# A windowed attention with a gated convolution layer behind it: the whole hand-laid order of its engines replaced

## The chip, the core and the metric

One core of a Trainium2 chip runs the kernel. The metric is the device time of one execution in microseconds, as the median of several. The core's engines run side by side, each through its own row of instructions in order: TensorE (PE) multiplies matrices, VectorE (DVE), ScalarE (ACT) and GpSimd (POOL) do the elementwise work, and SyncE (SP) issues the transfers between the memory and the chip. An instruction waits until what it reads has been written and what it overwrites has been read; everything behind it on its engine waits with it.

## The reference

```python
B, H, S, D = 8, 8, 576, 64
window = 64
scores = 1 / sqrt(D) * (q @ k.transpose)
scores = where((0 <= i - j) & (i - j < window), scores, -1e9)
scores = scores - max(scores)
attn = exp(scores); attn = attn / (sum(attn) + 1e-9)
x = (attn @ v).transpose(0, 2, 1, 3).reshape(B, S, H * D)       # 8 x 576 x 512

xp = pad(x, 4 rows of zeros in front)
gate_pre = sum(conv_w[k] * xp[:, k:k + S] for k in range(5))    # each of 512 channels by itself
gate = sigmoid(gate_pre)
y = (gate * (x @ w_val)) @ w_out                                # 8 x 576 x 512, float32
```

## The kernel before

**Tiles.** Heads go in groups of four (two pairs of heads), so that 16 groups w = 0 to 15 make the eight batches, two to a batch. A query block has 32 rows and sees 96 keys; a group is done in two pieces, g = 0 with five blocks and g = 1 with four, each piece in two halves hh. The 128 partitions hold four pieces of 32 queries.

**Operations and their names.** Every operation has a name, and the prediction uses these. `S(w,g)` are the scores of a piece on PE (line 521, 80 or 64 matmuls into PSUM tiles `s`). `M((w,g),hh)` adds the mask and takes the maximum on DVE (line 542, one instruction for each block). `X` is the exponential with the sum on ACT (line 552, one for each block). `R(w,g)` adds the sums up and takes the reciprocal on DVE (lines 560 and 561). `N` multiplies by it (line 573 on POOL or DVE, line 571 on ACT). `T` transposes on DVE into `pts` (line 579). `AVw_0` to `AVw_10` are the products with v on PE (line 610, into `av`), `EXi` copies a pair of heads from `av` to `x` (line 241 on ACT, line 244 on DVE; pairs 2w and 2w+1 belong to group w), `XHi` rounds it to the multiplier's format and `XLi` (POOL, line 760) keeps the rest. The convolution of pair i is `Ci_4` on ACT (line 811) and then `Ci_3` to `Ci_0` on DVE (line 808), which add the other taps into `gp`. For the pairs 0 and 1 it is done on PE instead: `Ki_0` and `Ki_1` (line 777, with diagonal matrices `DG0`, `DG1`, line 975, that POOL makes), copied out by `CC`. `SIGb` is the sigmoid of a batch on ACT (line 995). `Vb_h_jb` are the products with `w_val` on PE (line 852; each as three products of a high and a low part), `HF` (line 863, DVE) multiplies by the gate, `HH` and `HL` split the result, `O` are the products with `w_out` on PE (line 918), `EO` copies the result out and `DO` stores it.

**Weights.** The weights come as raw 64-bit words and are turned into float32 parts on the chip: for each of eight words `w0` to `w7`, and for the convolution's `cw`, a chain of operations `h k b c H p l r s` (lines 413 to 469; `b` is line 424, `r` 451, `s` 454). The prediction calls these the number operations. They fall in the first 70 us, and they stand between the attention's operations on the same engines.

**The order.** Nothing is scheduled at run time. A table `ORDER` lists all operations as words, and the function `placed` takes them in that sequence, with the engine behind a slash where an operation may run on more than one: each engine's row is the table's words for that engine. A word `*a+b` puts a + b matmuls that compute nothing (the spares, lines 1032 and 1034) ahead of the next operation:

```python
for word in ORDER:
    if word[0] == "*":
        spares = tuple(int(x) for x in word[1:].split("+"))
        continue
    name, _, e = word.partition("/")
```

Two PSUM tiles `s` hold the two halves of one piece of scores, so that the next `S` has to wait for both `M` of the one before. Two tiles `av` hold one group's products, and two tiles are shared by `K`, `V` and `O`. Loads stand in SP's row: `LQ` for q and k of a pair, `LV` for v of a group (eight transfers), `LW` for weight words (0.5 MB for `w_val`'s halves, 1 MB for `LW2` and `LW3` of `w_out`).

Of the kernel before, what the change touches and what calls it, by code (L numbers as in the profile page):

```python
# [45 lines left out]
    low='NNNNNAAAA',  # L46
)
# [7 lines left out]
X((1,0),1) w4u w3l/V R(0,1) w4k/V *1+0 S(1,1) N((0,1),1)/G T((0,0),1) M((1,1),1) N((0,1),0)/G T((0,1),1) w4b
M((1,1),0) T((0,1),0) *0+1 AV0_0 AV0_1 AV0_2 w3r/G w4c w3s/V w4p LQ4_0 LW3 LQ5_0 LV1 LW0_1 LQ6_0 LQ7_0 AV0_3
AV0_4 AV0_5 AV0_6 AV0_7 AV0_8 AV0_9 AV0_10 *0+3 S(2,0) X((1,1),0) w4l/V X((1,1),1) R(1,0) R(1,1) EX0/V DG1/G
w5h/A w4H N((1,1),0)/A EX1/A XH0/A w5u XH1/A N((1,0),1)/V w4r/V N((1,0),0)/V w4s/V M((2,0),0) T((1,0),1)
T((1,0),0) M((2,0),1) N((1,1),1)/G XL1 DG0/G XL0 FR0 FR1 K1_0 AV1_0 S(2,1) T((1,1),1) T((1,1),0) M((2,1),0)
M((2,1),1) K1_1 AV1_1 AV1_2 AV1_3 AV1_4 X((2,0),0) X((2,0),1) w1h/A X((2,1),0) CC1_0 X((2,1),1) AV1_5 AV1_6  # L60
AV1_7 AV1_8 AV1_9 AV1_10 w1k/V R(2,0) w5k/V w1b w5b w1c N((2,0),0)/V w5c w1p w5p T((2,0),0) R(2,1) K0_1 S(3,0)
w1H CC1_1 EX2/A EX3/A C2_4 XH2/G C3_4 CC0_1 XH3/A N((2,0),1)/A w1l/V C2_3 M((3,0),0) C3_3 M((3,0),1) K0_0
T((2,0),1) C3_2 S(3,1) M((3,1),0) M((3,1),1) LV2 LQ8_0 LQ9_0 LV3 S(4,0) X((3,0),0) w5H w5l/G w1r/G XL3
N((2,1),1)/G XL2 w1s/G w5r/G w5s/G N((2,1),0)/G LQ10_0 LQ11_0 V0_1_1_0 X((3,0),1) X((3,1),0) CC0_0 X((3,1),1)
w6h/A w7h/A C2_2 C3_1 C2_1 R(3,0) C2_0 T((2,1),1) C3_0 N((3,0),1)/G N((3,0),0)/G M((4,0),0) T((2,1),0) R(3,1)
M((4,0),1) w6k/V w7k/V w6b w7b SIG0_0 w6c w7c HF0_1_1 w6p w7p FX1 FX0 AV2_0 AV2_1 AV2_2 AV2_3 AV2_4 AV2_5 AV2_6
AV2_7 AV2_8 AV2_9 AV2_10 V0_0_2_0 S(4,1) V0_0_3_0 T((3,0),1) HF0_0_2 M((4,1),1) HF0_0_3 T((3,0),0) EX4/A w6u
EX5/A C5_4 w7u C4_4 LV4 LQ12_0 LQ13_0 N((3,1),0)/G HH0_1_1_0/G HL0_1_1_0 w6l/G HH0_0_2_0/A HH0_0_3_0/A HL0_0_3_0
HL0_0_2_0 w7l/G V0_0_0_0 C4_3 M((4,1),0) HF0_0_0 C5_3 C4_2 X((4,0),0) w6H w7H V0_1_0_0 V0_0_1_0 S(5,0) HF0_1_0
# [1014 lines left out]
```

## Time and profile before

| | |
|---|---|
| median of 3 runs | 329.29 us (329.21 to 330.62) |
| the profiled execution's own time | 331.42 us |
| its span from first to last instruction | 329.6 us |
| PE busy | 313.0 us, 95% |
| DVE busy | 260.3 us, 79% |
| ACT busy | 246.0 us, 75% |
| POOL busy | 174.0 us, 53% |
| mean granted clock of TensorE | 0.979 |

The profiled execution is 2.1 us longer than the median, and 1.8 us of its own time lie outside its span. The views are read in this order: the slices of the span, to see where PE is full and where it is not; PE's waits in the full part; the chain of work that ended last; then, in the part where PE is not full, the timelines of DVE, ACT and POOL, where each row is an instruction or a merged run of them, with the idle time ahead of it and what ended that in square brackets.

### The profile page before, as it was taken

The page shows a single profiled execution, that of the slowest core. Times are in us where ns is not written, and L with a number is a line of the kernel's source. Part 1 is how long each engine was busy: PE and PEld are TensorE (multiplying, and loading weights), DVE is VectorE, ACT ScalarE, POOL GpSimd, SP SyncE. Part 2 cuts the span into 40 slices and gives each one's busy share as a digit, 9 for nine tenths or more (in the row PEclk, how much of TensorE's full clock was granted, in tenths as well). Part 3 has the DMA queues.
Part 4 walks back from the last instruction along what each step waited for, and adds up shares of the span by engine and source line. Part 5 has one row for each costly group of instructions (what it writes and reads, how often), then busy time and mean ns, then how long its engine had stood idle before and what let it go on. Part 6 is the DMA issues. An engine that isn't in the chain of part 4 may idle for free.

```text
span 329.6 us, 14996 instructions
## 1 busy us (share of the span) xinstructions
PE 313.0 (95%) x6142; PEld 264.2 (80%) x6142; DVE 260.3 (79%) x992; ACT 246.0 (75%) x844; POOL 174.0 (53%) x227
## 2 busy tenths in 40 slices
PE   8966978899999999999999999999999999999996
PEld 3435766799788988798889988798889888989985
DVE  5799977999989999999989897799886948572301
ACT  3688969999999799999987677949797467552110
POOL 3436428579849860279504895148147721671710
PEclk9976879999999999999999999999999999999999
DMA  7969884260156654664536335550433111010022
GB/s 229 384 131 291 254 234 136 96 196 33 37 177 196 193 169 122 184 183 152 148 126 191 110 105 189 183 157 2 140 114 116 30 69 64 34 66 32 2 96 95
DMA packets 28228, 45.03 MB, mean 137 GB/s; under 512 B 3968, under 2 KB 15488, under 8 KB 28160
## 3 DMA queue, kind: packets, MB, share of 16 engines
q1 hardware_dynamic: 28160, 44.08, 43.3%
q8 instruction: 48, 0.79, 1.0%
q14 instruction: 20, 0.16, 0.2%
HBM read 34.62 MB, written 9.44 MB: 134 GB/s over the span
## 4 chain that ended last, share of the span: by engine, by line
PE 80%; DVE 13%; ACT 5%; issue 2%; POOL 0%; ACTq 0%; POOLq 0%
PE o L918 29%; PE v L852 27%; PE av L610 10%; PE s L521 8%; DVE p L542 4%; DVE gp L808 3%; PE g L777 3%; PE spare L1032 2%; ACT p L552 2%; DVE pts L579 2%; ACT p L571 1%; ACT h_hi L241 1%; PE spare L1034 0%; DVE w4a L424 0%; ACT L552 0%
## 5 line engine op out<-in xcount | busy, mean ns | idle before, releaser
L552 ACT ACTIVATE p<-p,nm 128x96 f32<-128x96 f32 x288 | 103.9, 363 | 7.7 <-DVE nm L542 7.5
L808 DVE SCALAR_TENSOR_TENSOR gp<-av,cw,gp 128x575 f32<-128x575 f32 (+3 forms) x120 | 93.4, 802 | 7.5 <-ACT gp L811 6.7
L852 PE MATMUL v<-xl,wv_hi 128*128 128x288 f32 x256 | 77.6, 303 | 0.7 <-ACT ot L241 0.7
L852 PE MATMUL v<-xh,wv_lo 128*128 128x288 f32 x256 | 75.4, 294 | 0.0
L852 PE MATMUL v<-xh,wv_hi 128*128 128x288 f32 x256 | 75.0, 293 | 0.0
L881 POOL TENSOR_TENSOR h_lo<-hf,h_hi 128x288 fp32r<-128x288 f32 (+2 forms) x80 | 53.9, 690 | 23.5 <-ACT h_hi L241 22.0
L542 DVE CUSTOM_DVE_ANT_0 p<-s,mask 128x96 f32<-128x96 f32 x288 | 54.8, 250 | 7.3 <-PE s L521 7.1
L918 PE MATMUL o<-wo_hi,h_lo 128*128 128x512 f32 (+1 forms) x148 | 59.6, 403 | 0.2 <-DVE hf L863 0.2
L918 PE MATMUL o<-wo_lo,h_hi 128*128 128x512 f32 (+1 forms) x148 | 57.7, 390 | 0.0
L918 PE MATMUL o<-wo_hi,h_hi 128*128 128x512 f32 (+1 forms) x148 | 57.6, 389 | 0.0
L552 ACT ACTIVATION_READ_ACCUMULATOR p<-p,nm 128x1 f32 x288 | 54.2, 188 | 0.0
L852 PEld LDWEIGHTS v<-xl,wv_hi 128*128 128x128 f32 x256 | 48.1, 188 | 4.0 <-ACT ot L241 1.1
L760 POOL TENSOR_TENSOR xl<-x,xh 128x576 fp32r<-128x576 f32 x32 | 46.0, 1445 | 9.9 <-ACT xh L241 9.6
L246 POOL CAST h_hi<-hf 128x288 fp32r<-128x288 f32 (+2 forms) x37 | 14.2, 392 | 66.1 <-DVE hf L863 57.6
L852 PEld LDWEIGHTS v<-xh,wv_hi 128*128 128x128 f32 x256 | 48.2, 188 | 0.6
L852 PEld LDWEIGHTS v<-xh,wv_lo 128*128 128x128 f32 x256 | 48.1, 188 | 0.0
L610 PEld LDWEIGHTS av<-pts,v 32*64 32x64 f32 x2560 | 36.5, 135 | 11.3 <-issue 5.3
L610 PE MATMUL av<-pts,v 32*64 32x96 f32 (+2 forms) x2560 | 39.6, 251 | 6.1 <-DVE pts L579 2.7
L521 PEld LDWEIGHTS s<-ktb,qtb 64*32 64x32 f32 x2304 | 30.7, 108 | 17.4 <-issue 14.5
L521 PE MATMUL s<-ktb,qtb 64*32 64x96 f32 x2304 | 38.9, 255 | 5.2 <-issue 2.7
L863 DVE TENSOR_TENSOR hf<-v,gp 128x288 f32<-128x288 f32 x64 | 28.2, 447 | 18.0 <-PE v L852 13.9
L573 POOL TENSOR_TENSOR p<-p,rc 128x384 f32<-128x384 f32 (+1 forms) x30 | 28.5, 955 | 20.9 <-DVE rc L561 17.6
(129 smaller groups left out, 443.6 us busy)
## 6 DMA issues: line engine op xcount, KB each, us to landing
out_dram<-ot SPq DMA_DIRECT2D x35, 256.0 KB, 2.5
qtb<-in_qT_dram SPq DMA_DIRECT2D x30, 288.0 KB, 4.2
ktb<-in_kT_dram SPq DMA_DIRECT2D x30, 288.0 KB, 4.5
v<-in_vw_dram SPq DMA_DIRECT2D x64, 96.0 KB, 3.3
v<-in_vw_dram SPq DMA_DIRECT2D x64, 80.0 KB, 3.3
st<-in_w_val_dram SPq DMA_DIRECT2D x4, 512.0 KB, 4.1
st<-in_w_out_dram SPq DMA_DIRECT2D x2, 1024.0 KB, 10.2
qtb<-in_qT_dram SPq DMA_DIRECT2D x2, 224.0 KB
```

Source lines behind the costliest of these rows:

```text
L246: COPY = {"A": scopy, "V": vcopy, "G": lambda out, in_: nc.gpsimd.tensor_copy(out=out, in_=in_)}
L521: nc.tensor.matmul(sp_t[m, hh][z * Q:z * Q + Q, t, :], lhsT=held("qt", i)[r, c:c + Q], rhs=held("kt", i)[r, c:c + KW], start=True, stop=True)
L542: nc.vector.tensor_tensor_reduce(out=pe[:, t, :], in0=sp_t[u][:, t, :], in1=mask_of(w, n0 + t), scale=-SCALE, scalar=3.0e38, op0=ALU.add, ...
L552: nc.scalar.activation(out=pe[:, t, :], in_=pe[:, t, :], func=AF.Exp, scale=-1.0, bias=nm[:, t:t + 1], accum_out=su[:, t:t + 1])
L573: MUL[e](out=pe, in0=pe, in1=rc.unsqueeze(2).broadcast_to([P, ng, KW]))
L610: nc.tensor.matmul(av_t[w, z // 2][hh * D:(hh + 1) * D, c + lo * Q:c + hi * Q], lhsT=v_t[w][z * Q:z * Q + Q, hh, m % 2, m // 2 - KEYS[th][ ...
L760: SUB[e](out=batch_tile(xl_t, "xl", b, F32R)[:, hp, :], in0=x_t[i // 2][:, i % 2, :], in1=xh_t[b][:, hp, :].bitcast(F32))
L808: nc.vector.scalar_tensor_tensor(out=acc, in0=av(i, 0, S - back), scalar=col, in1=acc, op0=ALU.mult, op1=ALU.add)
L852: nc.tensor.matmul(vp_t[u][:, 0:NH], lhsT=w[:, c, js], rhs=x[:, c, hs], start=(a + z == 0), stop=(a + z == NM - 1))
L863: nc.vector.tensor_mul(out=hf, in0=vp_t.pop(u)[:, 0:NH], in1=gp_t[b][:, jb, hs])
L881: SUB[e](out=h_lo[:, jb, dst:dst + hi - lo], in0=hf_t[u][:, lo:hi], in1=h_hi[:, jb, dst:dst + hi - lo].bitcast(F32))
L918: nc.tensor.matmul(op_t[key][:, 0:cs.stop - cs.start], lhsT=h[:, jb, col:col + P], rhs=w[:, jb, cs], start=(a + z == 0), stop=(a + z == NM ...
```

## The change

`CFG` gets a line `lane=(2200.0, 900.0, 700, 3350, 1.15)`, which nothing in the code reads. The table `ORDER` is replaced as a whole: the same operations, in another sequence, some on other engines. All line numbers behind `CFG` are higher by one. Of the table's first lines:

```diff
+    lane=(2200.0, 900.0, 700, 3350, 1.15),
 ...
-LW1_0 LC LQ0_0 LQ1_0 *5+0 S(0,0) w2h/A w2k/V cwh/A cwk/V w2b cwb w2c cwc w2p cwp w2l/V cwl/V M((0,0),0)
+LW1_0 LC LQ0_0 LQ1_0 LW0_0 LW1_1 w2h/V LQ0_1 LQ1_1 w2k/V cwh/A cwk/V w2b cwb w2c cwc cwH w2H w2p cwp w2l/V LQ2_0
+*4+0 S(0,0) cwl/G M((0,0),0) X((0,0),0) w2r/G LQ3_0 M((0,0),1) w0h/V w0k/V w2s/V w0b X((0,0),1) *2+0 S(0,1) w0c
```

The spares ahead of the first scores become four instead of five, those ahead of `S(1,0)` one instead of four. Up to the product `HF0_1_1` (the first with the gate of batch 0), DVE loses `cwl`, `cws`, `w4l`, `EX0` and three `N` of five blocks, and gets `w2h`, `w2s`, `w3r`, `w6p`, `DG0` and `EX1`. Over the whole run `N` stands on ACT 20 times (19 before), on POOL 36 times (30) and on DVE 8 times (15). On SP the 1 MB load `LW3` moves from between `LQ4` and `LQ5` to behind `LV1`, so that `LQ5` comes earlier.

On DVE, ahead of the first mask operation of piece (1,0) (`p_1_0`, line 542, line 543 after), stood before:

```order
L433 TENSOR_SCALAR w0m<-w0a 128x512
L439 SCALAR_TENSOR_TENSOR w0l<-st_225,w0m 128x512
L420 TENSOR_SCALAR w3m<-w3m 128x512
L560 TENSOR_REDUCE rc_0_263<-sums_64 128x10
L561 RECIPROCAL rc_0_263<-rc_0_263 128x10
L424 TENSOR_SCALAR w3a<-w3m 128x512
L454 TENSOR_TENSOR cl<-cwm,cwl 128x20
L429 SCALAR_TENSOR_TENSOR w3a<-st_139,w3a 128x512
L542 ISA p_1_0_323,nm_1_0_322<-s_1_0_286,mask_91 128x96
```

In this row, `p_1_0_323` belongs to the second piece, and `w0`, `w3` and `cl` are number operations. After:

```order
L425 TENSOR_SCALAR w0a<-w0m 128x512
L430 SCALAR_TENSOR_TENSOR w0a<-st_146,w0a 128x512
L561 TENSOR_REDUCE rc_0_298<-sums_64 128x10
L562 RECIPROCAL rc_0_298<-rc_0_298 128x10
L434 TENSOR_SCALAR w0m<-w0a 128x512
L421 TENSOR_SCALAR w3m<-w3m 128x512
L543 ISA p_1_0_319,nm_1_0_318<-s_1_0_258,mask_91 128x96
```

The low part of `w0`, the step `b` and `c` of `w3` went behind the mask operation, and `cl` went to POOL.

On ACT, around the last exponential of piece (1,1) in the second group (`p_1_1`, with the sums of its last four blocks), stood before:

```order
L552 ACTIVATE p_0_1_407,sums_66<-p_0_1_407,nm_0_1_406 128x96 x5
L465 ACTIVATE w4l<-st_131 128x512
L552 ACTIVATE p_1_0_478,sums_67<-p_1_0_478,nm_1_0_477 128x96 x4
L552 ACTIVATE p_1_1_469,sums_67<-p_1_1_469,nm_1_1_468 128x96 x4
L413 ACTIVATE w5m<-st_131 128x512
```

and after (line 572 is `N` on ACT, line 242 `EX0`):

```order
L553 ACTIVATE p_1_0_450,sums_67<-p_1_0_450,nm_1_0_449 128x96 x4
L466 ACTIVATE w4l<-st_131 128x512
L572 ACTIVATE p_0_0_382<-p_0_0_382,rc_0_475 128x96 x5
L572 ACTIVATE p_0_1_389<-p_0_1_389,rc_0_475 128x96 x5
L242 COPY x_594<-av_0_484 128x576
L553 ACTIVATE p_1_1_470,sums_67<-p_1_1_470,nm_1_1_469 128x96 x4
```

Two `N` and one `EX` went ahead of the last exponential, which `R(1,1)` on DVE needs.

On PE, at the second group's products (`av`, line 610, or 611 after) there stood before, behind the last score of the third group's second piece, the second half of the convolution of pair 1 (`g_1`, line 777, the operation `K1_1`):

```order
L521 MATMUL s_1_0_711<-ktb_82,qtb_78 32x96
L521 MATMUL s_1_1_712<-ktb_82,qtb_78 32x96
L777 MATMUL g_1_759<-x_651,dg 128x288 x5
L610 MATMUL av_0_701<-pts_0_681,v_521 64x96
L610 MATMUL av_0_701<-pts_1_679,v_521 64x96
```

and after, at the same scores:

```order
L522 MATMUL s_1_0_702<-ktb_82,qtb_78 32x96
L522 MATMUL s_1_1_703<-ktb_82,qtb_78 32x96
L611 MATMUL av_0_742<-pts_0_645,v_654 64x96
L611 MATMUL av_0_742<-pts_1_643,v_654 64x96
```

`K1_1` went behind `S(3,1)`; the first half, `K1_0`, which stood ahead of `AV1_0`, now stands behind `AV1_1`.

## Rows read from the trace of the kernel before

**Rows 1.** The page's busy tenths in 40 equal slices of the span: PE, DVE, and the granted TensorE clock in tenths.

```profile
PE   8966978899999999999999999999999999999996
...
DVE  5799977999989999999989897799886948572301
...
PEclk9976879999999999999999999999999999999999
```

**Rows 2.** PE's waits from 62.4 to 326.7 us: who waited for whom, us in total, times, the longest.

```profile
PE v L852 <- ACT ot L241: 0.7, 1, 0.7
PE av L610 <- DVE rc L560: 0.6, 1, 0.6
PE s L521 <- issue: 0.3, 1, 0.3
PE o L918 <- DVE hf L863: 0.2, 1, 0.2
```

**Rows 3.** The chain of work that ended last, in order of time: start, us, what.

```profile
39.16 2.62 PE g L777 x10
...
42.92 1.86 issue
44.78 1.76 PE av L610 x46
46.54 3.57 PE g L777 x10
50.11 1.20 PE s L521 x68
...
92.19 1.62 PE av L610 x78
```

**Rows 4.** DVE in order of time: start, us, line, operation, out<-in, count, and in brackets the idle time ahead of it and its releaser.

```profile
10.12 0.26 DVE L542 CUSTOM_DVE_ANT_0 p<-s,mask 128x96 f32<-128x96 f32 x1 [2.21 <-PE s L521]
...
48.34 0.82 DVE L808 SCALAR_TENSOR_TENSOR gp<-av,cw,gp 128x575 f32<-128x575 f32 x1 [2.12 <-ACT gp L811]
...
51.30 0.26 DVE L542 CUSTOM_DVE_ANT_0 p<-s,mask 128x96 f32<-128x96 f32 x1 [2.14 <-PE s L521]
...
65.99 0.45 DVE L863 TENSOR_TENSOR hf<-v,gp 128x288 f32<-128x288 f32 x1
```

**Rows 5.** ACT in order of time, at the end of the second group's first products and at `EX2`, `EX3` and the first taps `C2_4`, `C3_4`.

```profile
31.97 1.18 ACT L571 ACTIVATE p<-p,rc 128x96 f32<-128x96 f32 x4
33.04 0.63 ACT L241 COPY x<-av 128x576 f32<-128x576 f32 x1
...
46.45 1.18 ACT L241 COPY x<-av 128x576 f32<-128x576 f32 x2 [2.56 <-PE av L610]
47.52 1.45 ACT L811 ACTIVATE gp<-x,cw 128x576 f32<-128x576 f32 x2
```

**Rows 6.** The spares of line 1032 in the first 9 us (weight loads: shortest, median and longest in ns, first and last start), and the first scores behind them on PE.

```profile
L1032 PEld LDWEIGHTS spare<-ident x10: 190/337/337, 1.4 to 8.0; 128*128 128x128 f32 x10
8.90 1.20 PE L521 MATMUL s<-ktb,qtb 64*32 64x96 f32 x80
```

**Rows 7.** DVE in order of time: operations that leave DVE or are priced by these (`cwl`, `w0b`, `w3b`, `cws`, `w4b`, `w3s`, `w4l`, `EX0`, two `N`).

```profile
7.74 0.17 DVE L439 SCALAR_TENSOR_TENSOR cwl<-cwords,cwm 128x20 f32<-128x20 uint32 x1
...
12.82 0.43 DVE L424 TENSOR_SCALAR w0a<-w0m 128x512 int32<-128x512 int32 x1
...
15.77 1.17 DVE L424 TENSOR_SCALAR w3a<-w3m 128x512 int32<-128x512 int32 x1
16.85 1.24 DVE L454 TENSOR_TENSOR cl<-cwm,cwl 128x20 fp32r<-128x20 f32 x1
...
26.45 1.29 DVE L424 TENSOR_SCALAR w4a<-w4m 128x512 int32<-128x512 int32 x1
...
29.43 0.67 DVE L454 TENSOR_TENSOR wv_lo<-w3m,w3l 128x512 fp32r<-128x512 f32 x1
...
30.55 0.69 DVE L469 TENSOR_TENSOR w4l<-w4l,w4m 128x512 f32<-128x512 f32 x1
...
31.76 0.71 DVE L244 COPY x<-av 128x576 f32<-128x576 f32 x1
32.39 0.95 DVE L573 TENSOR_TENSOR p<-p,rc 128x480 f32<-128x480 f32 x1
...
33.86 0.65 DVE L573 TENSOR_TENSOR p<-p,rc 128x480 f32<-128x480 f32 x1
```

**Rows 8.** POOL in order of time beside two of the long rows of DVE above.

```profile
15.33 1.32 POOL L451 TENSOR_TENSOR w0m<-w0a,wv_hi 128x512 f32<-128x512 f32 x1 [4.52 <-ACT wv_hi L448]
...
26.19 1.26 POOL L451 TENSOR_TENSOR w3m<-w3a,wv_hi 128x512 f32<-128x512 f32 x1
```

**Rows 9.** The transposes of pieces of five blocks on DVE over the whole run: busy us, mean ns of one, idle before and its releaser.

```profile
L579 DVE STREAM_TRANSPOSE pts<-p 128x480 f32<-128x480 f32 x32 | 21.3, 667 | 0.2
```

**Rows 10.** `N` on POOL over the whole run, by shape: busy us, mean ns, idle before and its releasers.

```profile
L573 POOL TENSOR_TENSOR p<-p,rc 128x480 f32<-128x480 f32 x14 | 15.1, 1080 | 7.6 <-DVE rc L561 4.4 <-DVE rc L560 2.3 <-ACT p L552 0.8
L573 POOL TENSOR_TENSOR p<-p,rc 128x384 f32<-128x384 f32 x16 | 13.5, 846 | 13.3 <-DVE rc L561 13.3
```

**Rows 11.** The longest of DVE's waits for POOL over the whole run: us in total, times, the longest.

```profile
DVE hf L863 <- POOL h_lo L881: 1.5, 1, 1.5
```

**Rows 12.** The exponentials on ACT over the whole run: busy us, mean ns of one, idle before and its releaser.

```profile
L552 ACT ACTIVATE p<-p,nm 128x96 f32<-128x96 f32 x288 | 103.9, 363 | 7.7 <-DVE nm L542 7.5
```

More of the change, by code (lines that the diff above doesn't have):

```diff
@@ L46 @@
     low='NNNNNAAAA',
+    lane=(2200.0, 900.0, 700, 3350, 1.15),
 )
 ORDER = """
-LW1_0 LC LQ0_0 LQ1_0 *5+0 S(0,0) w2h/A w2k/V cwh/A cwk/V w2b cwb w2c cwc w2p cwp w2l/V cwl/V M((0,0),0)
-M((0,0),1) LW0_0 LQ1_1 LQ0_1 LW1_1 LQ2_0 cwH w2H X((0,0),0) X((0,0),1) w2r/G w2s/G w0h/V w0k/V w0b w0c w0p w0l/V
-w3h/A w0H w3k/V R(0,0) N((0,0),0)/A cwr/G w3b LQ3_0 LW2 LV0 *1+0 S(0,1) cws/V w3c M((0,1),0) M((0,1),1) w0r/G CF
-w3p T((0,0),0) *4+0 S(1,0) w0s/G N((0,0),1)/G X((0,1),0) X((0,1),1) w4h/A M((1,0),0) M((1,0),1) X((1,0),0) w3H
@@ L55 @@
[L55 to L69, printed above, removed]
@@ L150 @@
-O4096_0_0 EO3968_0/A HH7_1_0_0/A HL7_1_0_0 DO3968_0 DO3712_0 O4352_0_0 EO4096_0/A DO4096_0 O4480_0_0 EO4352_0/V
-DO4352_0 EO4480_0/A DO4480_0 O4224_0_0 EO4224_0/V DO4224_0 O4480_1_0 CB7 CB6 EO4480_1/A DO4480_1 FX15 FX14
+LW1_0 LC LQ0_0 LQ1_0 LW0_0 LW1_1 w2h/V LQ0_1 LQ1_1 w2k/V cwh/A cwk/V w2b cwb w2c cwc cwH w2H w2p cwp w2l/V LQ2_0
+*4+0 S(0,0) cwl/G M((0,0),0) X((0,0),0) w2r/G LQ3_0 M((0,0),1) w0h/V w0k/V w2s/V w0b X((0,0),1) *2+0 S(0,1) w0c
+w3h/A LW2 R(0,0) LV0 w0H w0p N((0,0),0)/A w3k/V M((0,1),0) M((0,1),1) N((0,0),1)/G cwr/G X((0,1),0) w0l/V w3b
@@ new lines @@
+*1+0 S(1,0) M((1,0),0) M((1,0),1) X((0,1),1) cws/G w0r/G w0s/G X((1,0),0) *1+0 S(1,1) R(0,1) T((0,0),0) w3c CF
+M((1,1),0) T((0,0),1) N((0,1),0)/G N((0,1),1)/G T((0,1),0) LQ4_0 X((1,0),1) w3p T((0,1),1) M((1,1),1) R(1,0)
+DG1/G LQ5_0 *3+0 AV0_0 AV0_1 w3H w4h/A w3l/V w4k/V AV0_2 AV0_3 X((1,1),0) w3r/V AV0_4 AV0_5 AV0_6 w4b AV0_7
+AV0_8 w4c w3s/V AV0_9 AV0_10 DG0/V w4p w4u N((1,0),0)/A N((1,0),1)/A EX0/A *1+0 S(2,0) X((1,1),1) T((1,0),1)
+T((1,0),0) XH0/G w4l/G R(1,1) LW0_1 LV1 M((2,0),0) w4H w5h/A N((1,1),1)/G X((2,0),0) w5k/V w4r/V M((2,0),1)
@@ new lines @@
+N((1,1),0)/G XL0 w5u X((2,0),1) EX1/V *2+0 S(2,1) FR0 FR1 M((2,1),0) AV1_0 AV1_1 K1_0 AV1_2 w4s/V X((2,1),0)
+XH1/G XL1 T((1,1),1) T((1,1),0) R(2,0) M((2,1),1) w1h/A N((2,0),1)/A X((2,1),1) AV1_3 AV1_4 AV1_5 AV1_6 w1k/V
+w5b w1b w5c AV1_7 AV1_8 AV1_9 AV1_10 w1c w5p w1p R(2,1) w1l/V K0_1 LW3 LQ6_0 LQ7_0 LV2 LQ8_0 LQ9_0 EX2/A w1H
+C2_4 w5H LV3 C2_3 T((2,0),1) XH2/G S(3,0) CC1_0 CC0_1 EX3/A N((2,0),0)/A K0_0 C2_2 M((3,0),0) M((3,0),1) C3_4
+XH3/A X((3,0),0) T((2,0),0) C3_3 XL2 w1r/G N((2,1),1)/G T((2,1),1) w1s/G w5l/G XL3 w5r/G w5s/G N((2,1),0)/G
@@ new lines @@
+S(3,1) K1_1 CC0_0 X((3,0),1) M((3,1),0) X((3,1),0) M((3,1),1) C2_1 C3_2 w6h/A CC1_1 FX1 FX0 S(4,0) C2_0 C3_1
+R(3,0) LQ10_0 LQ11_0 V0_1_1_0 C3_0 N((3,0),0)/G X((3,1),1) w7h/A AV2_0 AV2_1 M((4,0),0) T((2,1),0) AV2_2 SIG0_0
+R(3,1) w6k/V w7k/V w6b M((4,0),1) N((3,0),1)/G AV2_3 AV2_4 V0_0_2_0 AV2_5 S(4,1) AV2_6 AV2_7 AV2_8 AV2_9 w7b
+AV2_10 LQ12_0 w6c w7c w6p w6u N((3,1),0)/G HF0_1_1 V0_0_0_0 w6l/G EX4/A w6H HH0_1_1_0/A T((3,0),0) HF0_0_2
+M((4,1),0) T((3,0),1) HL0_1_1_0 V0_0_3_0 EX5/A HH0_0_2_0/A C5_4 HF0_0_0 w7p M((4,1),1) w7H C4_4 V0_1_0_0 C5_3
@@ new lines @@
+HL3_0_1_0 HL3_0_2_0 HL3_0_2_1 HL3_1_0_0 AV9_5 AV9_6 AV9_7 AV9_8 AV9_9 AV9_10 T((10,1),1) EX18/V V3_1_2_0
+M((12,0),1) HF3_1_2 HH3_1_2_0/G HL3_0_1_1 HL3_1_2_0 V3_1_3_0 V3_1_1_0 C18_4 R(11,1) C18_3 C18_2 HF3_1_3
+HH3_1_3_0/G EX19/A X((12,0),0) C19_4 X((12,0),1) O1792_0_0 N((11,0),0)/A HL3_1_3_0 HF3_1_1 HH3_1_1_0/G HL3_1_1_0
+O2048_0_0 C19_3 C19_2 XH18/G XH19/A C18_1 C19_1 T((11,0),0) C18_0 C19_0 XL19 N((11,0),1)/A EO1792_0/A S(12,1)
+SIG4_0 AV10_0 AV10_1 AV10_2 EO2048_0/V R(12,0) LQ28_0 DO1792_0 DO2048_0 LV11 AV10_3 XL18 N((12,0),0)/G XL16
@@ new lines @@
+X((14,1),0) HF4_1_1 T((13,0),1) X((13,1),1) C22_1 C23_2 M((14,1),1) O2432_0_0 EO2432_0/A HH4_1_1_0/A CB4 FX11
+FX10 S(15,0) O2304_0_0 C23_1 C22_0 R(14,0) R(13,1) N((13,1),0)/V C23_0 HH4_1_3_0/A HH4_1_2_0/A HL4_1_2_0
+N((14,0),0)/A HL4_1_3_0 SIG5_0 HL4_1_1_0 AV12_0 AV12_1 AV12_2 T((13,1),0) AV12_3 EO2304_0/V AV12_4 DO2432_0
+DO2304_0 LV13 AV12_5 AV12_6 AV12_7 AV12_8 AV12_9 AV12_10 O2560_0_0 M((15,0),1) T((14,0),0) N((13,1),1)/G
+T((13,1),1) HF5_0_0 M((15,0),0) EX24/A N((14,0),1)/V C24_4 HH5_0_0_0/A C24_3 EX25/A C25_4 EO2560_0/A C24_2
@@ new lines @@
+HL5_0_2_1 V5_1_1_0 HF5_1_1 T((14,0),1) EX27/A V5_1_2_0 HL5_1_3_0 O2944_0_0 C27_4 C26_4 C26_3 C27_3 C26_2 XH26/A
+HF5_1_2 T((14,1),1) C26_1 M((15,1),0) C26_0 T((14,1),0) XL24 XH27/G C27_2 C27_1 C27_0 T((15,0),1) XL27
+HH5_1_1_0/A HH5_1_0_0/A EO2944_0/A HH5_1_2_0/A XL26 HL5_1_2_0 CB5 FX12 FX13 HL5_1_1_0 HL5_1_0_0 O2816_0_0
+EO2816_0/A DO2816_0 DO2944_0 V6_0_0_0 SIG6_0 O3328_0_0 AV14_0 AV14_1 AV14_2 EO3328_0/V AV14_3 AV14_4 AV14_5
+AV14_6 AV14_7 AV14_8 AV14_9 AV14_10 EX28/A HF6_0_0 V6_0_2_0 HF6_0_2 EX29/V O3200_0_0 V6_0_3_0 XH28/A X((15,1),0)
@@ L152 @@
+HL7_0_0_1 HH7_1_2_0/G HL7_0_2_0 HL7_0_2_1 V7_1_0_0 HF7_1_1 HH7_1_1_0/A HL7_1_2_0 HL7_1_1_0 O3968_0_0 EO3968_0/A
+HF7_1_0 HH7_1_0_0/G HL7_1_0_0 O4480_0_0 EO4480_0/V DO3968_0 O4096_0_0 EO4096_0/A DO4480_0 O4352_0_0 DO4096_0
+O4224_0_0 EO4352_0/A DO4352_0 EO4224_0/V DO4224_0 CB6 FX14 CB7 FX15 O4480_1_0 EO4480_1/A DO4480_1
 """.split()
```

145 lines of the change are left out of this document (65 added, 80 removed).

## The prediction

> **What bounds the kernel now.** The slices come first. PE is busy nine tenths or more in every slice from the eighth on (from about 62 us), and below that in most slices before [rows 1]. PE's waits in the full part add up to 1.8 us in 264 us [rows 2], so from 62 us on the time is PE's own work, which both kernels have in the same amount. What an order can change is when this full part starts, and whether it stays full. So the second view is the chain of work before it. On PE it holds an "issue" of 1.86 us at 42.92, the products of the second group that end at 46.54, and a convolution of 3.57 us; then it goes over to DVE behind the scores at 50.11 and comes back to PE's products for good only at 92.19 [rows 3]. Between about 10 and 92 us DVE is nearly full too, as its own row of tenths shows [rows 1]. Hence the third view, DVE in order of time. The reader is to see its three long gaps: 2.21 us ahead of the first mask operation, 2.12 ahead of `C2_3` at 48.34, 2.14 ahead of the masks of group 3 at 51.30; and the end that I measure to, `HF0_1_1` at 65.99, which stands at the start of PE's full part [rows 4]. ACT explains the second: it sat 2.56 us until the second group's products were done at 46.45, copied two pairs, and only then took the two first taps, from 47.52 [rows 5].
>
> So the sum is made for DVE's row up to `HF0_1_1`: its work, its waits and what lengthens its instructions. A microsecond there is a microsecond at the end, as long as DVE and PE keep the pace behind it. The profiled execution took 331.42 us, 2.13 more than the median of 329.29; I take the difference over unchanged. About half a per cent (1.65 us, so 327.6 to 330.9) is what can be told from no change.
>
> **The parts.**
> 1. *DVE's work to that point.* Leaving: `cwl` 0.17, `cws` at the price of the same 20 columns 0.17, `w4l` 0.69, `EX0` 0.71, three `N` of 0.65 as the second one shows: 3.69 [rows 7]. Arriving: `w2h` and `w6p` at 0.43 (one tensor of 512 columns, as `w0b`), `w2s` and `w3r` at 0.67 (two tensors, as `w3s`), `EX1` 0.71, and `DG0`, 640 columns of two tensors, estimated as 0.67 x 640 / 512 = 0.84: 3.75 [rows 7]. Together **+0.1**.
> 2. *First scores.* One spare fewer ahead of `S(0,0)`. A spare shows as two matmuls; the last one's weights were loaded at 8.0 and the scores began at 8.90 [rows 6], so one spare is about **-0.9**. The gap of 2.21 covers it [rows 4]. If the loads of q and k land later than PE is ready, it is 0; the other spares stand where PE waits for DVE, and are taken at 0.
> 3. *The two waits of 2.12 and 2.14 [rows 4].* In the new row DVE masks piece (1,0) ahead of `w3b`, `w3c`, `w0l` and `cws`, so that exponentials, transposes and products of the first two groups come earlier, and `K1_1` (2.62 on PE at 39.16 [rows 3]) no longer stands ahead of the second group's products, nor `EX3` ahead of `C2_4`. The scores of group 3 have two convolution halves ahead of them instead of three. Both waits as they are go: **-4.3**. What is late next are the waits of part 4.
> 4. *New waits.* On ACT, two `N` and `EX0` now stand ahead of the exponential that `R(1,1)` waits for. Once the second `N` is done, ACT still has `EX0`, 0.63 [rows 5], and four exponentials of 0.363 [rows 12], 2.1 in all; DVE has two transposes meanwhile, some 0.6 each when they follow one another, at 0.667 [rows 9] a little more: a wait of 0.75 to 0.9. The same walk gives about 0.8 ahead of `C2_3` (behind `EX2`, a cast of a weight word and the tap on ACT), and about 0.5 ahead of the masks of `S(2,1)`. Together **+2.1**. Between 0 (DVE late itself) and 4.3 (the old waits in new places).
> 5. *DVE beside POOL.* Four of DVE's operations are much longer than their like: `w3b` 1.17 and `w4b` 1.29 against 0.43, `cws` 1.24 against 0.17, an `N` 0.95 against 0.65, 3.0 us in all [rows 7]. `w3b` began at 15.77, inside POOL's operation of 15.33 to 16.65, and ended after it; `w4b` began at 26.45, inside that of 26.19 to 27.45 [rows 8]. All four stand elsewhere now, or on POOL. I can't see from an order which others will begin inside a POOL operation. Ends: all of it gone (-3.0), as much again (0), or more (a rival below). I take half, **-1.5**, since number operations of the same kinds remain on both engines.
> 6. *PE at half clock.* The granted clock is 0.6 to 0.8 in the slices from 16 to 49 us [rows 1], and the same ten matmuls took 2.62 and, at the lower level, 3.57 [rows 3]. In the new order the second group's products end about 1.5 us before anyone on ACT takes them; an "issue" of 1.86 and 0.95 of slow clock would use up that and 1.3 more. I take **+0.5**, between 0 and 1.3.
> 7. *Behind the start.* At one place (`S(8,0)` to its masks, a product's `HF` and the next product) DVE has about 1.2 us more to do than PE beside it; before had 1.8 of such waits at other places [rows 2]. **+0.3**, between 0 and 1.2. The end of the run keeps its 12-matmul steps and its last copy: 0. On SP, `LQ5` comes ahead of the 1 MB of `LW3`, and `LW3` itself later; no row shows scores or a number operation held by either, and I count 0.
>
> Sum: 0.1 - 0.9 - 4.3 + 2.1 - 1.5 + 0.5 + 0.3 = -3.7 us: 327.7 for an execution like the profiled one, **325.6** for the median.
>
> **The rivals.**
> - *The waits only move.* DVE stays as short of work as it was, because what it waits for (ACT's exponentials, PE's products) is in the same chain: part 4 is 4.3 instead of 2.1. For it: ACT was full, too, between its waits, and its own work up to `C2_4` is the same. Against it: ACT's 2.56 us were a wait for PE [rows 5], which the new order shortens. -3.7 + 2.2 = -1.5: 327.8, which is within half a per cent.
> - *Nothing new gets in the way.* No overlap of DVE and POOL, no half clock on the path, no new wait behind: 0.1 - 0.9 - 4.3 + 2.1 - 3.0 = -6.0: 323.3. For it: all four long operations were accidents of two rows beside each other [rows 7, 8]. Against it: POOL has more work in the new rows, not less.
> - *More of DVE stands behind POOL.* Every number operation of DVE that begins inside one of POOL's is held to its end, as two of them visibly were [rows 7, 8]. If eight are hit instead of four, at the same 0.75 each, part 5 is +3.0 instead of -1.5: -3.7 + 4.5 = +0.8: 330.1. The Trainium skill, page "SBUF — State Buffer", section "SBUF: two separate sides", has a rule for this: the port pair that VectorE and GpSimd share is an exclusive lock, the instruction that starts first keeps it to its end, and the other one fully blocks. By that rule it is the number of overlaps and not POOL's busy time that counts, and the four long operations agree with it.
> - *Transposes behind POOL: slower.* `N` goes from DVE to POOL: 30 there before, 36 now, at 1.08 for five blocks and 0.85 for four [rows 10], against 0.65 on DVE [rows 7]; and the next transposes on DVE, then the products on PE, wait for it. Six more on the path at their full length, 6 x 0.97 = 5.8: -3.7 + 5.8 = +2.1: 331.4. From 3.7 us of such waits in all the change is no gain, from 5.4 it is slower by half a per cent. `N((1,1),1)` and `N((1,1),0)`, now one behind the other on POOL ahead of `T((1,1),1)`, are the first place. Against it: over the whole run the longest wait of DVE for POOL was 1.5 us, and for another operation [rows 11], with 30 of these `N` on POOL already.
>
> **How the numbers follow.** Chances: the forecast 0.45; nothing in the way 0.15; the waits only move 0.17; more behind POOL 0.08; transposes behind POOL 0.15. The forecast's own spread, from parts 4 to 6, is about 1.7 to either side, so that a tenth of its chance ends within half a per cent; the moved waits end within it more often than not. Faster by over 0.5%: 0.15 + 0.40 + 0.03 = 0.58. Slower: 0.11 of the transposes, 0.03 of the overlaps and 0.01 of the rest, 0.15. The rest, 0.27, is no change. The range goes from half a microsecond under the case at 323.3 to just above that at 330.1: 322.8 to 330.4; it leaves out most of the slower case and little else. On the forecast's side alone it would be 323.9 to 327.6.
>
> **What would show it.** In the trace after: the first mask operation near 9.2 us; DVE's gap ahead of `C2_3` under 1 us, and `C2_3` at 43 to 46 us instead of 48.34; a gap of 0.7 to 1 us ahead of `R(1,1)`; DVE operations over twice their like, counted: two if part 5 is right, none for the second rival, eight for the third; `HF0_1_1` between 60 and 64 us; PE idle under 3 us behind it. I am wrong if `HF0_1_1` comes earlier and the end doesn't (PE or DVE then gives it back behind 66 us, and part 7 failed), if `HF0_1_1` stands where it was (parts 3 and 4), or if the chain between 66 and 200 us goes through `N` on POOL and the transposes (the last rival).

## The result, and the profile after

The changed kernel is slower: 331.82 us (median of 19 runs, 328.88 to 333.47) against 330.00 us for the kernel before (19 runs beside it, 327.26 to 334.22); the ratio is 1.0052, 95% interval 1.0027 to 1.0077. The ratios here and below compare the runs of either kernel that lie within 1.5% of its fastest, so that they differ a little from the ratio of the medians. The forecast was 325.6 us, with a range of 322.8 to 330.4. The profiled execution took 333.47 us (span 331.7), 2.05 more than that of before.

The slices of the page come first, to be held against [rows 1]: PE, DVE and the granted clock in tenths.

```profile
PE   8685999899999999889999999999999999999996
...
DVE  5789799988998999877989896989786947563300
...
PEclk9978699799999999999999999999999999999999
```

PE's full part begins at much the same place, and the slice in which it begins (about 58 to 66 us) has a lower granted clock, 0.7. The next view is DVE in order of time, the answer to [rows 4]: start, us, line, operation, and in brackets the idle time ahead and its releaser.

```profile
10.27 0.26 DVE L543 CUSTOM_DVE_ANT_0 p<-s,mask 128x96 f32<-128x96 f32 x1 [2.19 <-PE s L522]
...
19.91 0.26 DVE L543 CUSTOM_DVE_ANT_0 p<-s,mask 128x96 f32<-128x96 f32 x1 [1.20 <-PE s L522]
...
35.33 0.26 DVE L543 CUSTOM_DVE_ANT_0 p<-s,mask 128x96 f32<-128x96 f32 x1 [1.29 <-PE s L522]
...
40.41 0.26 DVE L543 CUSTOM_DVE_ANT_0 p<-s,mask 128x96 f32<-128x96 f32 x1 [0.82 <-PE s L522]
...
48.33 0.82 DVE L809 SCALAR_TENSOR_TENSOR gp<-av,cw,gp 128x575 f32<-128x575 f32 x1
...
65.28 0.44 DVE L864 TENSOR_TENSOR hf<-v,gp 128x288 f32<-128x288 f32 x1
```

The first mask operation is not earlier (10.27 for 10.12): the scores ahead of it began earlier, at 8.04 for 8.90, but then PE stopped for k, as its timeline shows.

```profile
9.15 1.12 PE L522 MATMUL s<-ktb,qtb 64*32 64x96 f32 x72 [0.74 <-DMA ktb<-in_kT_dram]
```

The waits ahead of `C2_3` and of the masks of `S(3,0)` are gone, yet `C2_3` stands where it stood (48.33 for 48.34), and `HF0_1_1` came 0.7 us earlier instead of 4. Three other waits, 3.3 us in all, are for scores of PE; the old row had 0.8 us at the same masks. What PE waited for ahead of the second of them is the next view, PE in order of time at the first scores of group 2 (`S(2,0)`): "issue" is a wait for nothing that the profile shows.

```profile
33.21 2.08 PE L522 MATMUL s<-ktb,qtb 64*32 64x96 f32 x80 [3.58 <-issue]
```

The second reason is in DVE's instructions themselves. Here are those which the table further down counts as long, and under them POOL at the first five:

```profile
15.14 1.22 DVE L421 TENSOR_SCALAR w3m<-w3m 128x512 f32<-128x512 f32 x1
...
22.57 1.05 DVE L430 SCALAR_TENSOR_TENSOR w3a<-st,w3a 128x512 int32<-128x512 int32 x1
23.54 0.80 DVE L963 TENSOR_TENSOR cw<-ch,cl 128x20 f32<-128x20 f32 x1
...
31.72 0.89 DVE L434 TENSOR_SCALAR w4m<-w4a 128x512 int32<-128x512 int32 x1
...
36.22 1.21 DVE L421 TENSOR_SCALAR w5m<-w5m 128x512 f32<-128x512 f32 x1
...
41.12 1.23 DVE L455 TENSOR_TENSOR wo_lo<-w4m,w4l 128x512 fp32r<-128x512 f32 x1
...
47.38 0.99 DVE L440 SCALAR_TENSOR_TENSOR w1l<-st,w1m 128x512 f32<-128x512 uint32 x1
...
61.22 1.05 DVE L421 TENSOR_SCALAR w7m<-w7m 128x512 f32<-128x512 f32 x1
```

```profile
15.08 0.99 POOL L574 TENSOR_TENSOR p<-p,rc 128x480 f32<-128x480 f32 x1 [5.59 <-DVE rc L562]
...
22.24 2.06 POOL L574 TENSOR_TENSOR p<-p,rc 128x384 f32<-128x384 f32 x2 [1.06 <-ACT p L553]
...
31.36 0.96 POOL L247 CAST xh<-x 128x576 fp32r<-128x576 f32 x1 [5.70 <-ACT x L242]
...
35.75 1.40 POOL L761 TENSOR_TENSOR xl<-x,xh 128x576 fp32r<-128x576 f32 x1
```

Each begins inside an operation of POOL and ends just after it (POOL's row at 22.24 is two operations, of which the first ends at 23.07; the last three of DVE's began inside operations that ended at 41.80, 47.82 and 61.98). There are eight, and they cost 4.5 us over their like; before there were four, at 3.0 us [rows 7, 8]. Last, PE's waits from 66 us on (us in total, times, the longest), to be held against [rows 2], which begin at 62.4:

```profile
PE v L853 <- ACT ot L242: 1.2, 1, 1.2
PE v L853 <- ACT p L553: 0.9, 1, 0.9
PE s L522 <- DVE nm L543: 0.4, 1, 0.4
PE av L611 <- issue: 0.2, 1, 0.2
```

That is 2.7 us, where the kernel before had 1.2 from 66 us on. The largest, `V2_0_3_0` at 136.34, waited for a copy that ACT began at 135.73, behind five exponentials:

```profile
136.34 0.40 PE L853 MATMUL v<-xl,wv_hi 128*128 128x288 f32 x1 [1.15 <-ACT ot L242]
```

From `HF0_1_1` to the end the changed kernel took 2.7 us more than before. In the chain of work that ended last, twelve matmuls of `V` at the start of the full part, under the lower clock, show another piece of that; such a group takes 1.6 to 1.9 us later:

```profile
61.64 2.76 PE v L853 x12
```

### The profile page after: what moved, and what is told of

Same layout as the page of the kernel before. It is cut to its first block, busy times and chain, and to the rows that moved or that the text cites. A ratio compares the mean times of both kernels' runs of the same rounds, so it can differ in the third digit from the quotient of the medians.

```text
span 331.7 us, 15012 instructions
## 1 busy us (share of the span) xinstructions
PE 315.5 (95%) x6144; PEld 264.7 (80%) x6144; DVE 258.5 (78%) x985; ACT 245.6 (74%) x845; POOL 180.3 (54%) x241
## 4 chain that ended last, share of the span: by engine, by line
PE 75%; DVE 11%; ACT 5%; issue 3%; SPq 3%; DMA 3%; ACTq 0%
PE o L919 29%; PE v L853 28%; PE av L611 9%; PE s L522 8%; DVE p L543 3%; ACT p L553 2%; DMA ktb<-in_kT_dram 2%; DVE gp L809 2%; SPq L357 2%; PE spare L1033 1%; DVE pts L580 1%; DMA v<-in_vw_dram 1%; DVE wo_lo L455 1%; ACT h_hi L242 0%; SPq L336 0%
## 5 line engine op out<-in xcount | busy, mean ns | idle before, releaser
L853 PE MATMUL v<-xh,wv_hi 128*128 128x288 f32 x256 | 75.8, 296 | 0.0
L882 POOL TENSOR_TENSOR h_lo<-hf,h_hi 128x288 fp32r<-128x288 f32 (+2 forms) x80 | 53.6, 687 | 33.1 <-ACT h_hi L242 31.8
L574 POOL TENSOR_TENSOR p<-p,rc 128x384 f32<-128x384 f32 (+1 forms) x36 | 32.9, 923 | 49.8 <-DVE rc L562 44.2
L853 PEld LDWEIGHTS v<-xh,wv_hi 128*128 128x128 f32 x256 | 48.5, 189 | 1.4 <-issue 1.0
L853 PEld LDWEIGHTS v<-xh,wv_lo 128*128 128x128 f32 x256 | 48.5, 189 | 0.0
L522 PE MATMUL s<-ktb,qtb 64*32 64x96 f32 x2304 | 39.9, 258 | 7.9 <-issue 6.2
L611 PEld LDWEIGHTS av<-pts,v 32*64 32x64 f32 x2560 | 35.3, 131 | 7.8 <-issue 3.2
L611 PE MATMUL av<-pts,v 32*64 32x96 f32 (+2 forms) x2560 | 38.9, 245 | 1.7 <-issue 1.1
L580 DVE STREAM_TRANSPOSE pts<-p 128x384 f32<-128x384 f32 (+1 forms) x64 | 38.1, 611 | 1.3 <-ACT gp L996 0.7
```

Source lines behind the costliest of these rows:

```text
L522: nc.tensor.matmul(sp_t[m, hh][z * Q:z * Q + Q, t, :], lhsT=held("qt", i)[r, c:c + Q], rhs=held("kt", i)[r, c:c + KW], start=True, stop=True)
L574: MUL[e](out=pe, in0=pe, in1=rc.unsqueeze(2).broadcast_to([P, ng, KW]))
L580: nc.vector.transpose(out=pts_t[w, hh][:, n0 * KW:n1 * KW], in_=p_t.pop(u).rearrange("p t k -> p (t k)"))
L611: nc.tensor.matmul(av_t[w, z // 2][hh * D:(hh + 1) * D, c + lo * Q:c + hi * Q], lhsT=v_t[w][z * Q:z * Q + Q, hh, m % 2, m // 2 - KEYS[th][ ...
L853: nc.tensor.matmul(vp_t[u][:, 0:NH], lhsT=w[:, c, js], rhs=x[:, c, hs], start=(a + z == 0), stop=(a + z == NM - 1))
L882: SUB[e](out=h_lo[:, jb, dst:dst + hi - lo], in0=hf_t[u][:, lo:hi], in1=h_hi[:, jb, dst:dst + hi - lo].bitcast(F32))
```

## The experiments

Three theories were set up from this. **Theory 1**: the start is set by PE's own program. The profile has an instruction queue, which brought 48 packets of 16 KB over the 16 DMA engines that also move the data; if they are PE's program, a packet that comes late is the wait of 3.58 us. **Theory A/B**: the start gains nothing because the waits that the prediction took away were those of one execution (A), and because DVE is held by POOL more often (B). **Theory 3 or C**: the time is lost behind 66 us, at one copy (C). "Old" and "new" are the order before and the changed one; "start" is all up to `HF0_1_1`, "rest" what follows.

**One load moved.** In the changed order:

```diff
-R(1,1) LW0_1 LV1 M((2,0),0)
+R(1,1) LV1 LW0_1 M((2,0),0)
```

> The changed order, with one load moved: the 0.5 MB of weight words LW0_1 goes from ahead of the eight v loads LV1 to behind them. Theory 1 (PE's own program comes late: a 16 KB piece of its instructions queues behind the data transfers, and that is the 3.58 us ahead of S(2,0)): with less data in flight at 25 to 30 us the piece comes earlier, the wait falls below 1.5 us, S(2,0) starts at 29.5 to 31.5 instead of 33.21, C2_3 starts 1 to 2.5 us earlier than 48.33, and the time falls by 1 to 3 us against the changed order (ratio to the kernel before 0.996 to 1.003). Theory 2 (S(2,0) waits for q and k of pair 5, as it did in the kernel before, or for a fixed place in the row): S(2,0) stays within 0.4 us of 33.2 and the time stays at 1.005. Theory 3 (what is lost is lost behind 66 us): S(2,0) may move, the end stays at 1.005.

Measured: 331.57 us, ratio 1.0038 (1.0001 to 1.0076). The wait was 0.73 us, `S(2,0)` began at 29.95, `C2_3` at 46.36, `HF0_1_1` at 64.00. The rows were what theory 1 had said, and the time just missed its range. But later executions of the unmoved row had 0.68, 1.93, 2.48 and 2.67 us there, and five later kernels with the moved load 0.53 to 2.03: the wait varies by itself. It is shorter on average behind the moved load (1.2 us of six executions, for 2.3 of five), but the two overlap, so that the load isn't shown to set it.

**Starts and rests exchanged**, with the seam at `HF0_1_1`; the second kernel, for one, continues the changed order's first part with the old sequence:

```diff
 w7c w6p w6u N((3,1),0)/G HF0_1_1
-V0_0_0_0 w6l/G EX4/A w6H HH0_1_1_0/A T((3,0),0) HF0_0_2
+w7p V0_0_3_0 T((3,0),1) HF0_0_2 M((4,1),1) HF0_0_3 T((3,0),0)
```

> The words of the changed order up to HF0_1_1, then all others in the sequence and on the engines of the order before. Theory 3 (loss behind 66 us): 0.7 us earlier at HF0_1_1 stays to the end, ratio 0.996 to 0.999. Theory 1 (loss in the start, by the wait ahead of S(2,0) and the clock that follows from it): like the changed order less its new gaps behind, ratio 1.001 to 1.005.

> The reverse: the order before up to HF0_1_1, then the others as in the changed order. Theory 3: the new gaps behind 66 us come with it, 2 to 2.7 us, ratio 1.005 to 1.009. Theory 1: within 0.3% of the kernel before.

> The changed start with LW0_1 behind LV1, and the rest as in the order before. If theories 1 and 3 both hold, this has the gains of both: ratio 0.988 to 0.995, PE full from about 60 us. If theory 2 holds, it is as the run with the new start and the old rest.

Measured: new start and old rest 1.0040 (1.0004 to 1.0076); old start and new rest 1.0083 (1.0042 to 1.0125); new start with the load moved and old rest 1.0019 (0.9983 to 1.0055). The last was to gain 0.5 to 1.2% and gained nothing. By their ranges the first speaks for theory 1 and the second for theory 3; but the two losses would make 1.2% together, and the changed order, which has both parts, lost 0.5%. The second is the more telling for its trace, whose rows up to `HF0_1_1` are those of the kernel before: DVE waited neither ahead of `C2_3` nor ahead of the masks of `S(3,0)`, and `HF0_1_1` came at 62.64, 3.3 us before its place in [rows 4]. DVE's waits up to 66.5 us in it have no line for `gp`, which in the first trace waited 2.1:

```profile
DVE p L543 <- PE s L522: 3.3, 3, 1.4
DVE mask L278 <- POOL mask L274: 2.1, 1, 2.1
```

**Three local edits.** The copy first (C); number operations at four places put behind masks, transposes or a copy, of which the masks and the copy read PSUM, so that they don't meet POOL's operations (B), on top of the moved load; the load moved in the old order (A); and all three edits on the changed order.

```diff
-XL12 X((8,0),0) EO640_0/A
+XL12 EO640_0/A X((8,0),0)
```

```diff
-N((0,0),0)/A w3k/V M((0,1),0) M((0,1),1)
+N((0,0),0)/A M((0,1),0) M((0,1),1) w3k/V
-w3c CF M((1,1),0) ... w3p T((0,1),1) M((1,1),1)
+M((1,1),0) ... T((0,1),1) M((1,1),1) w3c CF w3p
-w4p ... T((1,0),1) T((1,0),0)
+... T((1,0),1) T((1,0),0) w4p
-w5k/V w4r/V M((2,0),1) ... EX1/V
+M((2,0),1) ... EX1/V w5k/V w4r/V
```

> The changed order with one word moved: the copy EO640_0 on ACT goes ahead of the five exponentials X((8,0),0). In the changed order PE waited 1.15 us for it ahead of V2_0_3_0 at 135. Theory C (this wait is a good part of what is lost behind 66 us): the wait goes, V2_0_3_0 takes 1.6 to 1.9 us instead of 3.0 after the product before it, PE's idle time from 100 us on falls from 2.3 to about 1, and the time falls by about 1 us (ratio 1.000 to 1.004). Rival (PE is held again at the next step, by the same ACT row): V2_0_3_0 earlier, but the ratio stays at 1.004 to 1.006 and PE waits 1 us more somewhere in 138 to 150.

> The changed order with LW0_1 behind LV1 as in the first run, and on DVE four number operations moved behind mask operations, transposes or a copy that read PSUM: w3k behind M((0,1),1); w3c, CF, w3p behind M((1,1),1); w4p behind T((1,0),0); w5k and w4r behind EX1. Same work on every engine. Theory B (eight of DVE's operations begin inside one of POOL's in the new start, 4.3 to 4.5 us, four in the old, 3.0 us): four or five remain, DVE's busy time up to HF0_1_1 falls from 56.0 to 54.0 to 55.0, and HF0_1_1 comes at 61 to 63 instead of 64.0; ratio 0.996 to 1.003. Rival (the start is set by PE's program pieces and the loads, and a shorter DVE only waits more): DVE's idle time grows by what its busy time loses, HF0_1_1 stays at 63.5 to 64.5, ratio 1.003 to 1.006.

> The order before with LW0_1 behind LQ7. Theory A (DVE's two waits of 2.12 and 2.14 in the trace of before follow from one late piece of PE's program ahead of the second group's products, which other executions of the same rows don't have; this is the second look at the old start): DVE has neither wait, HF0_1_1 comes at 62 to 64 instead of 65.99, and the median changes by less than 0.3%. Rival (the two waits belong to the old order): DVE waits about 2 us ahead of C2_3 and of the masks of S(3,0) again, HF0_1_1 at 65.5 to 66.5.

> The changed order with all three edits: LW0_1 behind LV1, the number operations behind the masks, EO640_0 first. If theories B and C hold, their gains add up: HF0_1_1 at 61 to 63, no wait at V2_0_3_0, ratio 0.992 to 0.999. If the rivals hold, 1.001 to 1.005.

Measured: copy first 1.0031 (0.9983 to 1.0080). The wait is gone and does not come back: PE's waits from 66 us on in that kernel are one line.

```profile
PE s L522 <- DVE nm L543: 0.7, 2, 0.3
```

Masks first: 0.9981 (0.9934 to 1.0027), six long operations of 3.7 us instead of eight, DVE busy 55.4 us up to `HF0_1_1` at 61.40. The rows went the way of theory B, but not as far as it said (four or five long operations, 54 to 55 us busy). Three other executions of this start had the same six long operations and put `HF0_1_1` at 62.17, 63.06 and 64.25, so that the end doesn't show it beyond doubt. The load moved in the old order spoiled itself: ACT stood 6.09 us until those weight words had come, and `HF0_1_1` fell to 68.68; the ratio of 1.0015 (0.9968 to 1.0062) says nothing on theory A.

```profile
45.19 0.66 ACT L414 ACTIVATE w1m<-st 128x512 f32<-128x512 f32 x1 [6.09 <-DMA st<-in_w_val_dram]
```

All three edits: 0.9950 (0.9916 to 0.9984), the only kernel that came out clearly faster than the one before; it was run a second time below.

**Further executions.** The kernel before unchanged, twice, each a single execution; the masks first with the old rest; all three edits again.

> The kernel before, unchanged, for another look at its start. Theory A (of DVE's waits of 2.12 and 2.14, the first follows from a piece of PE's program that came late in that execution): PE's wait ahead of the second group's products is under 1 us or ends earlier than 44.8, DVE's wait ahead of C2_3 is under 1 us, HF0_1_1 at 62 to 64.5. Rival (the waits belong to the order): both waits at about 2 us, HF0_1_1 at 65.5 to 66.5.

> The same kernel a third time. Theory A: HF0_1_1 differs from the first look by over 1 us, and with it PE's waits for its program in the first 50 us, while DVE's four long operations stay the same four. Rival: as in the first trace, within 0.5 us.

> The new start with LW0_1 behind LV1 and the number operations behind the masks, then the old sequence from HF0_1_1 on. If the new rest with EO640_0 moved is as good as the old rest, this is like the run with all three edits, 0.993 to 0.998; if the old rest is better, 0.988 to 0.993; if the gain of that run came from the new rest, 0.998 to 1.002.

> All three edits a second time, to see whether the version holds: 0.992 to 0.999 if it does.

Measured: the first of the two repeats the order of waits of [rows 4] (`HF0_1_1` at 65.92; the pair is 1.4 and 2.7 us for 2.1 and 2.1), the second doesn't (63.94). DVE's waits up to 66.5 us in the first of them:

```profile
DVE p L542 <- PE s L521: 5.8, 4, 2.7
...
DVE gp L808 <- ACT gp L811: 1.4, 1, 1.4
```

and in the second, where `gp` has no line:

```profile
DVE p L542 <- PE s L521: 4.5, 4, 2.0
```

So the rival was right for one execution, theory A for the other, though not in that the long operations stay the same four: a fifth came. The pair goes with a stop of PE: in the two traces that have it, PE stopped at "issue" within the second group's products, until 44.8 and 44.4 us, and the granted clock was at its lower level (1.2 GHz) from 45.0 to 48.4 and 45.1 to 48.5. The other four traces of the old start have neither that clock there nor a stop of over 0.2 us. The masks with the old rest gave 1.0037 (1.0001 to 1.0074), worse than each thing it was to tell apart; the three edits gave 1.0010 (0.9984 to 1.0037), outside what was expected if they hold. No version is shown to be faster than the kernel before.

**A square on one chip**: old and new start with the new rest, each with and without the copy moved (edit as above).

> The old start, the new rest, EO640_0 ahead of X((8,0),0). If the copy is the main loss behind 66 us: PE's lost time between 130 and 160 us is 2.3 to 2.9 us instead of 4.3 as with the old start and the new rest before, and the time is 0.3 to 0.6% below that of the same order without the edit. Rival (the loss is spread over the new rest): the lost time comes back within 30 us, and the two times agree within 0.2%.

> The old start and the new rest a second time, as the partner of the run above: ratio 1.004 to 1.009.

> The changed order itself, on the same chip: ratio 1.003 to 1.007 as measured. If the new start by itself gains nothing (theory A and B together), it agrees with the old start and the new rest within 0.25%; if it gains what the prediction said, it is 1% below that.

> The changed order with EO640_0 first, the partner of the run above: 0.3 to 0.6% below it if the copy is the main loss, within 0.2% if not.

| | new rest | new rest, copy first |
|---|---|---|
| old start | 1.0022 (0.9973 to 1.0071) | 1.0007 (0.9976 to 1.0039) |
| new start | 1.0035 (1.0003 to 1.0067) | 1.0010 (0.9980 to 1.0040) |

The start makes no difference that shows (0.13% and 0.03%, the new one the slower), where the prediction needed about 1.2%. The medians of all twelve runs differ more, but in opposite directions: 331.9 us with the old start and 330.6 with the new one in the first column, 329.7 and 330.3 in the second. The second run of the old start with the new rest fell short of its first (1.0083) and of what was expected (1.004 to 1.009), which shows how far a ratio can move. The copy takes back 0.15 and 0.25%, less than the 0.3 to 0.6% expected and within the intervals. In the traces its wait is plain: `V2_0_3_0` waited 0.8 to 1.2 us in all six kernels that had the new rest at that place unedited, and PE had no such wait there in the five with the edit.

Counted from the traces, PE's idle time from `HF0_1_1` to the end agrees with that: 1.8 us on average with the old rest (seven executions), 2.6 with the new one (six), 1.6 with the copy first (five). The time of that stretch does not: 265.0, 265.8 and 265.7 us, each within a spread of 2 to 3 us. So the copy is shown to cost PE its wait; that the end comes earlier without it is not shown.

What the traces of the two unedited starts show together is the next table (old: [rows 4], its two repeats and the three with the new rest; new: the changed kernel, its repeat, two with the copy first, one with the old rest), counted from the traces: DVE's busy and idle time up to `HF0_1_1`, its operations over 0.15 us longer than their like, and when `HF0_1_1` began.

```text
            traces HF0_1_1 (mean)         DVE busy        DVE idle        long operations
old start   6      62.64 to 65.99 (64.15) 54.7 to 55.5    6.3 to 10.4     4 or 5, 2.9 to 3.8 us
            mean                          55.16           8.19            3.4 us
new start   5      62.04 to 65.28 (63.46) 55.7 to 56.3    5.1 to 8.3      8 in each, 4.1 to 4.6 us
            mean                          56.04           6.63            4.4 us
```

The new start waits 1.6 us less and works 0.9 us more: 0.7 us is what it gains on average, within a spread of 3 to 4 us from execution to execution, so that even the 0.7 is not shown beyond doubt.

## Why the prediction was wrong

**Step 5 failed first.** It had the right mechanism with the wrong sign: the four long operations did go, and eight others came. Instead of -1.5 it was +1.5 in the two first traces and +1.0 on average. That is 2.5 to 3 us of the 3.3 by which `HF0_1_1` fell short: parts 1 to 6 make 4.0 us earlier, and 0.7 came. The rival that counted eight hits was right in its count, though they cost less than its 0.75 each, and by the sign that the prediction gave (over twice their like) they are five. Their number hardly varies from execution to execution (eight in each of the five, 4.1 to 4.6 us; one of the eight is another operation in the first trace), and it fell to six when the order was edited: it goes with the order. The rule that the prediction draws on there from the Trainium skill, "SBUF — State Buffer", section "SBUF: two separate sides", agrees in this: each of the eight ended 0.04 to 0.55 us after POOL's operation. The section limits the rule to VectorE operations in a two-port mode or with two inputs in SBUF, a condition that the prediction left out; so not every overlap counts, and the masks in the last section bear that out.

**Step 3 was sized on one execution.** Both waits went in the first trace, as it said. But the pair belongs to two of six executions of the old order, those in which PE stopped within the second group's products; a third had 1.1 us of the second wait. Over the six they make some 1.6 us, not 4.3. A saving was counted against one trace that other executions of the kernel before don't owe.

**Step 4** had 2.1 and got 3.3 (1.20, 1.29, 0.82), of which 0.8 stood in the old row: its size was near, its places were not. There was none at `R(1,1)`, where DVE was late itself, and none at `C2_3`; only the 0.82, ahead of the masks of `S(2,1)`, is one it named. All three are waits for scores. **Step 6** is behind one of them: it allowed an "issue" wait 1.3 us, and 3.58 came, not at the second group's products but ahead of `S(2,0)`. Of that DVE lost 1.29; in the run with one load moved, where PE waited 0.73, `M((2,0),0)` began at 33.50 instead of 35.33, held by DVE's own row. **Step 2** gave nothing in the first trace: the spare was worth its 0.9 on PE, but the scores then stopped 0.74 us for k, and the masks began 0.15 us later. The step had named this case, and took it not to come. Over the executions it came out at half: the first mask stood at 9.41 on average in five of the new start, at 9.85 in six of the old. Three of those five had the stop for k, none of the six; which of the moved loads makes it was not tried. **Step 1** was right: busy time less the long operations is 51.8 before and 51.7 after.

**Step 7 failed behind the start.** It gave 0.3 us and at most 1.2; in the two first traces it was 2.7. Counted from the traces, PE was idle 1.3 us longer behind `HF0_1_1` (2.6 for 1.3) and busy 1.4 us longer. The copy behind the exponentials is 1.15 of the idle time, and the experiments show that wait come and go with the copy's place; it stands in the stretch of `S(8,0)` that the step named, but on ACT and not on DVE. About 1 us of the busy time is the lower clock in 62 to 66 us (2.76 us for twelve matmuls that otherwise take 1.6 to 1.9). It stands there in two of the five executions of the new start, and in 60 to 69 us in three of the six of the old one, so it is not shown to be of the order. The rest stays open.

Profile against profile this adds up: DVE's idle time -2.1, its busy time +1.4, the rest +2.7, in all +2.0. For the medians it does not: by the averages over the traces the start gains 0.7 us and the new rest costs 0.8, so that about nothing would be expected (an estimate from few executions), and +1.8 (0.9 to 2.5 by the interval), then +1.2 (0.1 to 2.2) was measured. What makes the remaining 1 to 2 us stays open; single executions, 3 us apart in their start alone, can't place it. The slower rival, transposes behind POOL's `N`, did not come: no line of DVE's waits in the changed kernel names POOL's `N`.

## What to carry to other kernels

A wait in one profiled execution is an estimate of one: before its removal is counted, look whether a second execution of the same rows has it, above all when it ends at an "issue". A new order of two engines that hold each other up, as POOL does DVE here, has to be searched for pairs that overlap, since those that go are replaced by others. And a copy that frees the one buffer which PE needs next goes ahead of a long run of exponentials, even when its own due time seems far: here PE's wait went with it, though the gain in time is not clear of the spread.

## What the runs showed of the hardware that was not expected

PE resumed 1.4 to 1.6 us after the end of a 16 KB packet of the instruction queue, in the six traces that were read for it (PE had stopped at `S(2,0)` or its spare). Times in us:

```text
kernel                    packet ends   PE resumes   wait before
changed                   31.78         33.21        3.58
changed, again            29.84         31.45        2.67
new start, old rest       28.82         30.38        2.48
copy first                28.43         30.01        0.68
one load moved            28.55         29.95        0.73
before, third trace       32.21         33.61        2.01
```

The packet ended anywhere from 28.4 to 31.8 us in executions of the same rows. That the DMA load sets this was tried with one load and not shown. The traces hold 27 more stops at "issue" of over 0.6 us behind 20 us, and all of them end 1.2 to 1.6 us after the end of such a packet; with 48 packets in some 330 us this is hardly chance. The stops of 1.0 to 2.6 us ahead of `S(1,0)`, at 15 to 20 us, do not follow it. That the packets are PE's program is read from this match, the trace does not name what they carry.

Which of DVE's operations POOL holds could be seen too. The long ones up to `HF0_1_1`, four before and eight after, all work on SBUF tensors alone. Of the 288 mask operations, which read one operand from PSUM, 178 began inside an operation of POOL in the trace before, and none was longer than the others; of 64 transposes, which have one input, in SBUF, 41 began inside one, and none was longer.
